# Sharing the 96-wide tails of gate and up between one full tile and a two-column-tile rest, in an attention plus GeGLU kernel on one core

## Chip, cores and metric

One core of a Trainium2 chip. The metric is the device time in microseconds (us) of one execution. Every run carries a state: fast, or slow when the granted TensorE clock was lower. A "ratio" is the mean time of one kernel's fast runs over the mean of the other's fast runs in the same rounds, so it is not quite the ratio of the medians that are quoted beside it. Intervals are 95%.

## The reference

```python
# x: 1 x 2048 x 512 bf16; 32 heads of 16; window of 8 keys, every second one; Df = 1376
xn = layernorm(x)                                   # no gain, no bias
q, k, v = split(xn @ wqkv)
attn = softmax(mask(q . k[pos - {0,2,...,14}]) / 4) # 8 logits for each position and head
a = (attn . v[same positions]) @ wo
g, u = xn @ w_gate, xn @ w_up                       # 2048 x 1376 each
out = x + a + (gelu_tanh(g) * u) @ w_down
```

The 1376 hidden columns are ten tiles of 128 and a tail of 96. The tail is what the change is about.

## The kernel before

The program is a list of tasks (engine, priority, what it reads and writes). A list scheduler at build time puts them into one static order for each engine, so a changed priority can move work that the change does not touch. The 2048 rows are four blocks of 512. Here are the parts that the argument needs, cut.

```python
# weights: gate and up whole (1376 columns), down in 10 tiles and a 96-row tail
Wg = sb("Wg", [128, 4, DF], BF);  Wu = sb("Wu", [128, 4, DF], BF)
Wd = sb("Wd", [128, NJ, 512], BF)                      # NJ = 11
# ... loads on the queue of the SP engine ...

for j in range(NJ):                                    # per block b of 512 rows
    M = 128 if j < 10 else DF - 1280                   # 96 in the tail
    # PE: gate and up, four 512-column matmuls each, into one PSUM bank each
    for kt in range(4):
        e.matmul(PS[0:M, bank], lhsT=Wx[:, kt, j*128:j*128+M], rhs=xnT[:, slot, kt, :],
                 start=(kt == 0), stop=(kt == 3))
    # ACT: gelu(gate) -> GG, copy of up -> UU;  DVE: HT[j] = GG * UU
    # all of them with priority fb + j
# ...
# down projection of row tile ti: 4 matmuls of Wo on the attention output, 11 of Wd
for j in js:
    K = 128 if j < 10 else DF - 1280
    e.matmul(PS[:, bank], lhsT=HT[0:K, slot, j, rows], rhs=Wd[0:K, j, c0:c1], ...)
# first row tile of a block: tiles 0..7 in one task, 8..10 in a second one
ja, jb = list(range(8)), list(range(8, NJ))
G.order_after(t_a, t_of["fu%d_10" % b])                # behind the last tail of up
```

Four other pieces:

```python
# DVE, LayerNorm: the second step of a tile (XIN is scaled in place), bf16 to bf16
e.tensor_scalar(out=XIN[...], in0=XIN[...], scalar1=rstd[...], ..., op0=ALU.mult)
# SP queue: the normalised x of the next blocks is transposed by DMA
e.dma_start_transpose(xnT[:, slot, :, o:o+128], XIN[:, slot, t2, :])           # "trx"
# SP queue: softmax weights go out to memory and come back in another layout
e.dma_start(pt_scratch..., PB...)                                             # "ss", 4 stores
e.dma_start(PT[...], pt_scratch...)                                           # "sl", 1 load
# DVE: PVS = BS (values) * PT;  PE: sums of PVS over heads with 32-wide column tiles ("value group")
```

Of the kernel before, what the change touches and what calls it, by code (L numbers as in the profile page):

```python
# [647 lines left out]
def d_mm(n, cnt=1):  # L648
    return cnt * max(64, n) * 0.4167e-3


def d_act(n):
    return 0.16 + 0.00085 * n
# [10 lines left out]
def bass_parallel_sum__sliding_local_dilated__glu_gated_geglu__prompt_kernel(nc, A_x, A_wqkv, A_wo, B_x, B_w_gate, B_w_up, B_w_down, out, dbg=None, cfg=None):  # L664
# [3 lines left out]
    NQT = cfg.get("NQT", 2)  # L668
    NXT = cfg.get("NXT", 3)
    NPROD = cfg.get("NPROD", 4)  # L670
    JA = cfg.get("JA", 8)
    NMS = cfg.get("NMS", 2)
    NDE = cfg.get("NDE", 1)
    NPB = cfg.get("NPB", 1)
# [25 lines left out]
    NJ = 11  # L700
# [4 lines left out]
    with contextlib.ExitStack() as es:  # L705
        block = es.enter_context(nc.Block())

        def sb(name, shape, dt):
            return es.enter_context(nc.sbuf_tensor(name, shape, dt))

        Wqkv = sb("Wqkv", [128, 4, 1536], BF)
        Wg = sb("Wg", [128, 4, DF], BF)
        Wu = sb("Wu", [128, 4, DF], BF)
        Wd = sb("Wd", [128, NJ, 512], BF)
        Wo = sb("Wo", [128, 4, 512], BF)
        xnT = sb("xnT", [128, NXT, 4, 512], BF)
# [83 lines left out]
        I_VD = Item("VD")  # L800
        I_PD = Item("PD")
        I_out = Item("out")

        PC = -1000
        PC2 = cfg.get("PC2", 8)
# [17 lines left out]
               rd=[I_E8f], wr=[I_E8], prio=PC2)  # L823
        G.task("pool", "c_zpad", 0.1, lambda e: e.memset(zpad[:, :], 0.0), wr=[I_zpad], prio=PC2)
        G.task("pool", "c_ktpad", 0.15, lambda e: e.memset(KT[:, :, 0:16], 0.0), wr=[(I_KT, "pad")], prio=PC2)
        G.task("pool", "c_e4a", 0.3, lambda e: e.tensor_tensor(
            out=E4f[:, :], in0=cf[:, 0:32], in1=cf[:, 32:64], op=ALU.add), rd=[I_cf], wr=[I_E4f], prio=PC2)
        G.task("pool", "c_e4b", 0.3, lambda e: e.tensor_tensor(
# [31 lines left out]
        for i, nm in enumerate(("q", "k", "v")):  # L860
# [2 lines left out]
                    Wqkv[:, :, i * 512:(i + 1) * 512],  # L863
                    A_wqkv[:, i * 512:(i + 1) * 512].rearrange("(k p) n -> p k n", p=128))
            t_ld["w" + nm] = G.task("sp", "ld_w" + nm, 0, mk(), wr=[(I_wq, nm)], prio=-900 + i, nbytes=512 * 1024)
        WCH = cfg.get("WCHUNK", [11])
        wch_of = {}
        j0 = 0
        for ci, nj in enumerate(WCH):
            c_lo = j0 * 128  # L870
            c_hi = min(DF, (j0 + nj) * 128)
            for j in range(j0, j0 + nj):
                wch_of[j] = ci
            for (nm, Wx, I_w, src) in (("g", Wg, I_wg, B_w_gate), ("u", Wu, I_wu, B_w_up)):
                def mk(Wx=Wx, src=src, c_lo=c_lo, c_hi=c_hi):
                    return lambda e: e.dma_start(
                        Wx[:, :, c_lo:c_hi], src[:, c_lo:c_hi].rearrange("(k p) n -> p k n", p=128))
                t_w = G.task("sp", "ld_w%s%d" % (nm, ci), 0, mk(), wr=[(I_w, ci)], prio=R_WG + 2 * ci + (nm == "u"),
                       nbytes=(c_hi - c_lo) * 1024)
                t_w.deps.add(t_ld["wk"])  # L880
                t_ld[nm] = t_w
            j0 += nj
        t_w = G.task("sp", "ld_wd0", 0, lambda e: e.dma_start(
            Wd[:, 0:10, :], B_w_down[0:1280, :].rearrange("(j p) n -> p j n", p=128)),
            wr=[(I_wd, 0)], prio=R_WD, nbytes=1280 * 1024)
        G.order_after(t_w, t_ld["u"])
        t_w2 = G.task("sp", "ld_wd1", 0, lambda e: e.dma_start(
            Wd[0:96, 10, :], B_w_down[1280:1376, :]), wr=[(I_wd, 1)], prio=R_WD + 1, nbytes=96 * 1024)
        G.order_after(t_w2, t_w)
        for d4 in range(4):  # L890
            def mk(d4=d4):
# [134 lines left out]
        for b in range(NB):  # L1026
# [264 lines left out]

            it_ht = Item("ht%d" % b, P_ht, "ht")
            fb = FFN_BASE + b * FFN_STEP
            for j in range(NJ):
                M = 128 if j < 10 else DF - 1280
                it_g = Item("g%d_%d" % (b, j), P_ps, "ffn")
                it_u = Item("u%d_%d" % (b, j), P_ps, "ffn")
                it_gg = Item("gg%d_%d" % (b, j), P_gg, "gg")
                it_uu = Item("uu%d_%d" % (b, j), P_uu, "uu")
                for (nm, Wx, I_w, it_p) in (("g", Wg, I_wg, it_g), ("u", Wu, I_wu, it_u)):  # L1300
                    def mk_f(Wx=Wx, it=it_p, j=j, M=M, itx=XTI[b]):
                        def f(e):
                            ins = None
                            for kt in range(4):
                                ins = e.matmul(PS[0:M, 512 * it.slot:512 * it.slot + 512],  # L1305
                                               lhsT=Wx[:, kt, j * 128:j * 128 + M], rhs=xnT[:, itx.slot, kt, :],
                                               start=(kt == 0), stop=(kt == 3))
                            return ins
                        return f
                    t_of["f%s%d_%d" % (nm, b, j)] = G.task("pe", "f%s%d_%d" % (nm, b, j), d_mm(512, 4), mk_f(),  # L1310
                           rd=[XTI[b], (I_w, wch_of[j])], wr=[it_p], prio=fb + j,
                           mode="f")

                def mk_gl(it=it_g, ito=it_gg, M=M):
                    return lambda e: e.activation(  # L1315
                        out=GG[0:M, ito.slot, :], in_=PS[0:M, 512 * it.slot:512 * it.slot + 512],
                        func=ACTF.Gelu_apprx_tanh)
                t_of["gelu%d_%d" % (b, j)] = G.task("act", "gelu%d_%d" % (b, j), d_act(512), mk_gl(), rd=[it_g], wr=[it_gg], prio=fb + j,
                       table="gelu")

                def mk_ue(it=it_u, ito=it_uu, M=M):
                    return lambda e: e.activation(  # L1322
                        out=UU[0:M, ito.slot, :], in_=PS[0:M, 512 * it.slot:512 * it.slot + 512], func=ACTF.Identity)
                G.task("act", "uev%d_%d" % (b, j), d_act(512), mk_ue(), rd=[it_u], wr=[it_uu], prio=fb + j)

                def mk_h(ig=it_gg, iu=it_uu, ito=it_ht, j=j, M=M):
                    return lambda e: e.tensor_tensor(  # L1327
                        out=HT[0:M, ito.slot, j, :], in0=GG[0:M, ig.slot, :], in1=UU[0:M, iu.slot, :], op=ALU.mult)
                G.task("dve", "h%d_%d" % (b, j), d_dve(512, 0.52), mk_h(), rd=[it_gg, it_uu], wr=[(it_ht, j)],
                       prio=fb + j)  # L1330

            for ti in range(4):
                t = 4 * b + ti
# [7 lines left out]
                for ci, (c0, c1) in enumerate(cparts):  # L1341
# [5 lines left out]
                    def mk_acc(js, wo, stop, ti=ti, it=it_acc, ith=it_ht, ito=it_ot, c0=c0, c1=c1, CW=CW):  # L1347
                        def f(e):
# [3 lines left out]
                                               lhsT=OT[:, ito.slot, dq, ti * 128:(ti + 1) * 128],  # L1352
                                               rhs=Wo[:, dq, c0:c1], start=(dq == 0), stop=False)
                            for j in js:
                                K = 128 if j < 10 else DF - 1280
                                ins = e.matmul(PS[:, 512 * it.slot:512 * it.slot + CW],  # L1356
                                               lhsT=HT[0:K, ith.slot, j, ti * 128:(ti + 1) * 128],
                                               rhs=Wd[0:K, j, c0:c1], start=False, stop=(stop and j == js[-1]))
                            return ins
                        return f  # L1360
                    acc_kw = dict(mode="f", util=CW / (CW + 128.0))
                    if ti == 0:
                        ja, jb = list(range(JA)), list(range(JA, NJ))
                        t_a = G.task("pe", "acca" + sfx, d_mm(CW, 4 + len(ja)), mk_acc(ja, True, False),
                               rd=[(it_ht, j) for j in ja] + [I_wd, it_ot, I_wo], wr=[it_acc],
                               prio=base + 60, **acc_kw)
                        G.order_after(t_a, t_of["fu%d_10" % b])
                        G.task("pe", "accb" + sfx, d_mm(CW, len(jb)), mk_acc(jb, False, True),
                               rd=[(it_ht, j) for j in jb] + [I_wd, it_acc], wr=[it_acc],
                               prio=base + 59.5, **acc_kw)  # L1370
# [82 lines left out]
```

## Time and profile before

| | before |
|---|---|
| time, median of 3 runs | 201.35 us (201.34 to 201.56) |
| span of the profiled run, granted clock | 199.7 us, 1.000 |
| busy: PE, DVE, ACT, POOL | 194.4, 149.2, 104.7, 10.4 us |
| longest wait of PE after the first 8 us | 0.5 us, near 92 us |

A line of a timeline reads: start in us, length in us, engine, source line, operation, what is written from what is read, tile of PE (contracted rows by output columns), moving operand, count. A bracket gives the idle time just before and what ended it. Lengths of matmuls are modelled, so PE is read from one start to the next. The prediction below shows the lines that carry its argument. One more stretch is from PE's timeline: the one hole.

```profile
91.40 1.03 PE L1305 MATMUL PS<-xnT,Wg 128*128 128x512 bf16 x4
92.89 1.05 PE L1274 MATMUL PS<-PVS,E 128*32 128x512 bf16 x16 [0.46 <-ACT UU L1322]
94.03 0.61 PE L1151 MATMUL PS<-PROD,E 128*32 128x512 bf16 x8
```

From 91.40 to 92.89 is 1.49 us for a group that needs 0.86 and a switch of 0.10. From 92.89 to 94.03 is 1.14 us for 16 matmuls that need 0.87. So 0.53 us (0.46 of it is the idle time in the bracket) and 0.27 us are lost here.

The second is VectorE's timeline in the start, where nothing but LayerNorm of the first rows can run:

```profile
9.05 0.35 DVE L972 TENSOR_SCALAR XIN<-XIN,rstd 128x512 bf16<-128x512 bf16 x1
...
10.59 0.35 DVE L972 TENSOR_SCALAR XIN<-XIN,rstd 128x512 bf16<-128x512 bf16 x1
```

These are the scalings of the third and fourth row tile, 0.35 us each. PE's first matmuls read what they write.

### The profile page before, as it was taken

The page shows a single profiled execution, that of the slowest core. Times are in us where ns is not written, and L with a number is a line of the kernel's source. Part 1 is how long each engine was busy: PE and PEld are TensorE (multiplying, and loading weights), DVE is VectorE, ACT ScalarE, POOL GpSimd, SP SyncE. Part 2 cuts the span into 40 slices and gives each one's busy share as a digit, 9 for nine tenths or more (in the row PEclk, how much of TensorE's full clock was granted, in tenths as well). Part 3 has the DMA queues.
Part 4 walks back from the last instruction along what each step waited for, and adds up shares of the span by engine and source line. Part 5 has one row for each costly group of instructions (what it writes and reads, how often), then busy time and mean ns, then how long its engine had stood idle before and what let it go on. Part 6 is the DMA issues. An engine that isn't in the chain of part 4 may idle for free.

```text
span 199.7 us, 3150 instructions
## 1 busy us (share of the span) xinstructions
PE 194.4 (97%) x1192; PEld 89.5 (45%) x1192; DVE 149.2 (75%) x230; ACT 104.7 (52%) x171; POOL 10.4 (5%) x32
## 2 busy tenths in 40 slices
PE   7899999999999999998999999999999999999994
PEld 2694344444443444443344444333444444444483
DVE  3889999889998997699996529999792986222231
ACT  4477469775667302677563036874892007767000
POOL 6520010101000010000000000000000000000000
PEclk9999999999999999999999999999999999999999
DMA  5999998898659426355931244377112440010121
GB/s 146 360 402 375 276 102 170 210 256 144 184 144 218 50 93 144 119 141 151 216 76 53 82 133 105 95 163 167 53 38 67 119 121 26 0 53 5 37 81 41
DMA packets 33055, 27.03 MB, mean 135 GB/s; under 512 B 9392, under 2 KB 31504, under 8 KB 33040
## 3 DMA queue, kind: packets, MB, share of 16 engines
q1 hardware_dynamic: 33040, 26.83, 53.8%
q8 instruction: 9, 0.15, 0.3%
q14 instruction: 6, 0.05, 0.1%
HBM read 19.99 MB, written 5.26 MB: 126 GB/s over the span
## 4 chain that ended last, share of the span: by engine, by line
PE 93%; DMA 2%; ACT 2%; DVE 1%; SPq 1%; issue 0%; DVEq 0%
PE PS L1305 37%; PE PS L1356 19%; PE PS L1089 17%; PE PS L1351 7%; PE PS L1151 4%; PE PS L1274 4%; PE PS L1045 3%; DMA XIN<-in_A_x_dram 2%; ACT L1315 1%; ACT OT L1285 1%; ACT UU L1322 0%; PE PS L997 0%; SPq L910 0%; DVE st L925 0%; ACT GG L1315 0%
## 5 line engine op out<-in xcount | busy, mean ns | idle before, releaser
L1305 PE MATMUL PS<-xnT,Wu 128*128 128x512 bf16 (+1 forms) x176 | 45.2, 380 | 0.0
L1305 PE MATMUL PS<-xnT,Wg 128*128 128x512 bf16 (+1 forms) x176 | 45.1, 379 | 0.0
L1356 PE MATMUL PS<-Wd,HT 128*128 128x512 bf16 (+3 forms) x198 | 41.3, 356 | 0.0
L1255 DVE TENSOR_TENSOR PVS<-BS,PT 128x2048 bf16<-128x2048 bf16 x32 | 37.1, 1216 | 4.2 <-DMA PT<-pt_scratch 3.5
L1135 DVE TENSOR_TENSOR PROD<-QT,KT 128x2048 bf16<-128x2048 bf16 x32 | 36.9, 1216 | 0.5 <-ACT KT L1106 0.3
L1089 PE MATMUL PS<-xnT,Wqkv 128*128 128x512 bf16 x160 | 35.9, 379 | 0.0
L1315 ACT ACTIVATE GG<-PS 128x512 bf16<-128x512 f32 (+1 forms) x44 | 26.5, 602 | 15.5 <-PE PS L1305 11.8
L1322 ACT ACTIVATE UU<-PS 128x512 bf16<-128x512 f32 (+1 forms) x44 | 26.5, 602 | 9.8 <-PE PS L1305 9.5
L1327 DVE TENSOR_TENSOR HT<-GG,UU 128x512 bf16<-128x512 bf16 (+1 forms) x44 | 17.2, 417 | 15.5 <-ACT UU L1322 15.5
L1356 PEld LDWEIGHTS PS<-Wd,HT 128*128 128x128 bf16 (+1 forms) x198 | 19.4, 98 | 18.7
L1305 PEld LDWEIGHTS PS<-xnT,Wg 128*128 128x128 bf16 (+1 forms) x176 | 17.1, 100 | 21.6 <-issue 2.5
L1305 PEld LDWEIGHTS PS<-xnT,Wu 128*128 128x128 bf16 (+1 forms) x176 | 16.6, 100 | 22.9 <-issue 3.4
L1376 DVE TENSOR_TENSOR OB<-PS,XR 128x512 bf16<-128x512 f32 (+1 forms) x18 | 11.3, 628 | 19.7 <-PE PS L1356 18.5
L1089 PEld LDWEIGHTS PS<-xnT,Wqkv 128*128 128x128 bf16 x160 | 15.4, 98 | 19.0 <-issue 0.4
L1351 PE MATMUL PS<-Wo,OT 128*128 128x512 bf16 (+1 forms) x72 | 16.8, 355 | 0.0
L1285 ACT ACTIVATE OT<-PS 128x512 bf16<-128x512 f32 x16 | 8.7, 595 | 15.3 <-PE PS L1274 15.3
L1106 ACT ACTIVATE KT<-PS 128x512 bf16<-128x512 f32 x12 | 7.2, 597 | 13.3 <-PE PS L1089 13.3
L1099 ACT ACTIVATE QT<-PS 128x512 bf16<-128x512 f32 x12 | 7.2, 596 | 12.8 <-PE PS L1089 12.6
L925 DVE BATCH_NORM_STATS2 st<-XIN 128x6 f32<-128x512 bf16 x16 | 10.7, 685 | 3.7 <-DMA XIN<-in_A_x_dram 3.7
L1113 ACT ACTIVATE VT<-PS 128x512 bf16<-128x512 f32 x16 | 9.6, 598 | 4.7 <-PE PS L1089 4.7
L942 POOL TENSOR_TENSOR sq<-ve,mhalf 128x2 bf16<-128x2 f32 (+1 forms) x10 | 6.7, 666 | 68.5 <-DVE ve L936 68.5
L1351 PEld LDWEIGHTS PS<-Wo,OT 128*128 128x128 bf16 x72 | 6.9, 97 | 7.2 <-issue 0.4
(53 smaller groups left out, 117.1 us busy)
## 6 DMA issues: line engine op xcount, KB each, us to landing
BS<-vt_scratch SPq DMA_DIRECT2D x64, 128.5 KB, 3.1
vt_scratch<-VT SPq DMA_DIRECT2D x16, 128.0 KB
XR<-in_A_x_dram SPq DMA_DIRECT2D x16, 128.0 KB, 2.1
XIN<-in_A_x_dram SPq DMA_DIRECT2D x7, 256.0 KB, 6.1
out_dram<-OB SPq DMA_DIRECT2D x14, 128.0 KB, 2.0
Wqkv<-in_A_wqkv_dram SPq DMA_DIRECT2D x3, 512.0 KB, 4.2
Wg<-in_B_w_gate_dram SPq DMA_DIRECT2D x1, 1376.0 KB
Wu<-in_B_w_up_dram SPq DMA_DIRECT2D x1, 1376.0 KB, 11.2
```

The costliest lines, as they stand in the source:

```text
L925: return lambda e: e.bn_stats(out=st[:, t, :], in_=XIN[:, it.slot, t2, :])
L1089: ins = e.matmul(PS[:, 512 * it.slot:512 * it.slot + HWD], lhsT=lhsT, rhs=xnT[:, itx.slot, kt, c0:c0 + HWD], start=(kt == 0), stop=(kt == 3))
L1135: return lambda e: e.tensor_tensor(out=PROD[:, it.slot, :, :], in0=bass.AP(QT, (itq.slot * 4 + g) * 512, [[NQT * 4 * 512, 128], [0, 4], [1 ...
L1255: return lambda e: e.tensor_tensor(out=bass.AP(PVS, (ito.slot * 2 + half) * 2048, [[NPVS * 4096, 128], [512, 4], [128, 4], [1, 128]]), in0 ...
L1285: return lambda e: e.activation(out=OT[:, ito.slot, dq, :], in_=PS[:, 512 * it.slot:512 * it.slot + 512], func=ACTF.Identity)
L1305: ins = e.matmul(PS[0:M, 512 * it.slot:512 * it.slot + 512], lhsT=Wx[:, kt, j * 128:j * 128 + M], rhs=xnT[:, itx.slot, kt, :], start=(kt = ...
L1315: return lambda e: e.activation(out=GG[0:M, ito.slot, :], in_=PS[0:M, 512 * it.slot:512 * it.slot + 512], func=ACTF.Gelu_apprx_tanh)
L1322: return lambda e: e.activation(out=UU[0:M, ito.slot, :], in_=PS[0:M, 512 * it.slot:512 * it.slot + 512], func=ACTF.Identity)
L1327: return lambda e: e.tensor_tensor(out=HT[0:M, ito.slot, j, :], in0=GG[0:M, ig.slot, :], in1=UU[0:M, iu.slot, :], op=ALU.mult)
L1351: ins = e.matmul(PS[:, 512 * it.slot:512 * it.slot + CW], lhsT=OT[:, ito.slot, dq, ti * 128:(ti + 1) * 128], rhs=Wo[:, dq, c0:c1], start=( ...
L1356: ins = e.matmul(PS[:, 512 * it.slot:512 * it.slot + CW], lhsT=HT[0:K, ith.slot, j, ti * 128:(ti + 1) * 128], rhs=Wd[0:K, j, c0:c1], start ...
L1376: return lambda e: e.tensor_tensor(out=OB[:, ito.slot, 0:CW], in0=PS[:, 512 * it.slot:512 * it.slot + CW], in1=XR[:, itx.slot, c0:c1], op= ...
```

## The change

Intent: a 96-wide tile costs PE as much as a 128-wide one. Gate's 96 tail columns and 32 of up's fill one full tile. Up's other 64 columns are a rest, which is run as two 64-wide column tiles side by side, each on half of the 512 rows. That is meant to take half a group's time. The tail is given its turn after the fifth pair of tiles instead of at the end. The tail of the down weights lies in rows 32 to 127, so that its hidden values stand at the partitions where the products leave them; 32 rows of zeros fill it up.

```diff
+        Wt = sb("Wt", [128, 4, 192], BF)              # gate tail 96 + up 32 | up 64
+        G.task("pool", "c_wdz", ..., lambda e: e.memset(Wd[0:32, 10, :], 0.0), prio=PC2 + 20)
+        G.task("pool", "c_htz", ..., lambda e: e.memset(HT[0:32, :, 10, :], 0.0), prio=PC2 + 20)
...      # three loads for Wt behind those of Wg and Wu, which shrink to 1280 columns
-            Wd[0:96, 10, :], B_w_down[1280:1376, :]
+            Wd[32:128, 10, :], B_w_down[1280:1376, :]
...
-            for j in range(NJ):
+            for j in range(NJ - 1):
...
+                    for kt in range(4):                # full tail tile, priority fb + 4.5
+                        e.matmul(PS[:, bank], lhsT=Wt[:, kt, 0:128], rhs=xnT[:, slot, kt, :], ...)
+                    for kt in range(4):                # rest, priority fb + 4.5
+                        for c in range(2):
+                            e.matmul(PS[64*c:64*c+64, 256 columns], lhsT=Wt[:, kt, 128:192],
+                                     rhs=xnT[:, slot, kt, 256*c:256*c+256], tile_position=(0, 64*c))
+                # ACT: one gelu over all 128 partitions; no copy of up's tail
+            for (nm, p0, n, g0, c0, c1, it_s) in (("a", 0, 32, 32, 0, 512, it_g),
+                                ("b", 0, 64, 64, 0, 256, it_u), ("c", 64, 64, 64, 256, 512, it_u)):
+                    # DVE: HT[g0:g0+n, 10, c0:c1] = GG[g0:g0+n, c0:c1] * PS[p0:p0+n, ...]
...
-                                K = 128 if j < 10 else DF - 1280
-                        ja, jb = list(range(JA)), list(range(JA, NJ))
+                        ja, jb = [0, 1, 2, 3, 4, 5, 6, 7, 10], [8, 9]
-                        G.order_after(t_a, t_of["fu%d_10" % b])
+                        G.order_after(t_a, t_of["fu%d_9" % b])
```

## The prediction

> **What bounds the kernel now.** I read the page's busy shares first, then the chain of work that ended last, then the longest waits, then each engine's timeline.
>
> ```profile
> PE 194.4 (97%) x1192; PEld 89.5 (45%) x1192; DVE 149.2 (75%) x230; ACT 104.7 (52%) x171; POOL 10.4 (5%) x32
> ...
> PE 93%; DMA 2%; ACT 2%; DVE 1%; SPq 1%; issue 0%; DVEq 0%
> ```
>
> TensorE is busy for 97% of the span and is 93% of the chain. A busy PE is no proof by itself, because matmul ends are modelled, so the waits of PE have to be looked at:
>
> ```profile
> PE PS L853 <- POOL wsrc L806: 1.4, 1, 1.4
> PE PS L1045 <- ACT xnT L1008: 0.5, 1, 0.5
> PE PS L1274 <- ACT UU L1322: 0.5, 1, 0.5
> PE PS L997 <- DVE XIN L972: 0.2, 1, 0.2
> ```
>
> These are all the waits of PE: 2.6 us, and 2.1 us of them lie in the first 8 us. From then until the last matmul at 197 us the PE stream has one hole of 0.5 us, near 92 us. So the time is decided by how many PE slots the kernel issues and by what a switch between two kinds of matmul costs. Both are read from start-to-start times in PE's timeline:
>
> ```profile
> 19.87 1.90 PE L1305 MATMUL PS<-xnT,Wg 128*128 128x512 bf16 x8
> 21.70 0.62 PE L1151 MATMUL PS<-PROD,E 128*32 128x512 bf16 x8
> 22.25 1.04 PE L1305 MATMUL PS<-xnT,Wg 128*128 128x512 bf16 x4
> ...
> 38.24 1.03 PE L1305 MATMUL PS<-xnT,Wu 128*128 128x512 bf16 x4
> 39.10 1.03 PE L1305 MATMUL PS<-xnT,Wg 128*96 128x512 bf16 x4
> 39.96 1.03 PE L1305 MATMUL PS<-xnT,Wu 128*96 128x512 bf16 x4
> 40.83 6.21 PE L1089 MATMUL PS<-xnT,Wqkv 128*128 128x512 bf16 x28
> ```
>
> Three readings. A full group of four 512-column matmuls takes 39.10 - 38.24 = 0.86 us, 216 ns each. The two 96-wide tail groups take 0.86 and 0.87 us: a tail that is a quarter narrower costs exactly as much as a full tile. And eight matmuls on 32-wide column tiles start at 21.70 and give way at 22.25, 0.55 us: at 216 ns each one after the other they would need 1.73 us, so four of them run side by side and the pure streaming is two rounds, 0.43 us.
>
> **The price of a switch.** From 19.87 to 22.25 is 2.38 us for eight full matmuls (1.73) and those two rounds (0.43): the rest, 0.22 us, is going to column tiles and back, about 0.10 in and 0.12 out.
>
> **What the Trainium skill says.** (1) "TensorEngine Tiling (Array Packing)", section Key Properties: a change of the tiling mode drains the TensorE, while different tiles execute in parallel. The trace agrees in both: 0.22 us for the two changes, and four abreast. It has no case of two 64-wide tiles, which the change uses. (2) "TensorE: Matmul & The Clock Gate", section "Step-by-step: what each phase is for": weight loading scales with the column count and the row count doesn't matter. So padding the down tail from 96 to 128 rows should be free; the trace has 381 ns for the 96-row down matmul and 379 for the 128-row one, 98 ns for both weight loads. (3) "VectorE: DVE Perf Modes", section "What auto-detection actually checks": the packed 2x mode needs every tensor to be 16-bit. The trace agrees: the 512-element product of two bf16 tiles takes 417 ns, the 512-element add with an f32 PSUM operand 687 ns. (4) "DMA: Bandwidth & Descriptors", Specifications: at least 512 B for line rate. The new tail loads have rows of 192, 64 and 128 B; no row of the trace before isolates what such a load costs.
>
> ```profile
> L1327 DVE TENSOR_TENSOR HT<-GG,UU 96x512 bf16<-96x512 bf16 x4 | 1.7, 418 | 2.6 <-ACT UU L1322 2.6
> L1376 DVE TENSOR_TENSOR OB<-PS,XR 128x512 bf16<-128x512 f32 x14 | 9.6, 687 | 15.2 <-PE PS L1356 15.1
> L1376 DVE TENSOR_TENSOR OB<-PS,XR 128x256 bf16<-128x256 f32 x4 | 1.7, 424 | 4.6 <-PE PS L1356 3.4 <-DMA out_dram<-OB 1.2
> L1322 ACT ACTIVATE UU<-PS 96x512 bf16<-96x512 f32 x4 | 2.4, 592 | 0.9 <-PE PS L1305 0.8
> ```
>
> **The change part by part, for each of the four blocks.**
> PE, removed: eight 96-wide matmuls of 512 columns, 8 x 0.216 = 1.73 us. PE, added: one full group (gate's 96 columns and 32 of up), 4 x 0.216 = 0.86 us, and eight matmuls of 64 columns x 256 elements on two column tiles. If the pair runs side by side, that is four rounds at half of 0.216 (the 256-wide down matmuls come 15 in 1.64 us, 109 ns each, so halving the length does halve the pitch): 0.44 us. Plus two mode switches, 0.22 us, unless the group lands next to another column-tiled group; then those switches are paid already. Net: 1.73 - 0.86 - 0.44 - 0.22 = 0.21 us saved where the rest stands alone, 0.43 where it has a tiled neighbour.
> Where will it stand? It has its turn after the fifth pair of gate and up. In block 0 (about 30 us) and in block 3 (about 172 us) the neighbours are full matmuls: 2 x 0.21. In block 1 (about 63 us) and block 2 (about 139 us) the small logit groups of the next block are interleaved there, so a shared switch is possible: 2 x 0.21 to 2 x 0.43. Sum 0.84 to 1.28 us; I take 1.0 us. All of it lies on the path, as PE has no idle time to hide it in.
> ACT: four copies of up's tail go (4 x 0.59 = 2.4 us of 104.7). ACT is 52% busy and mostly waits for PE, so worth nothing by itself.
> DVE: per block one 418 ns product goes; three with a PSUM operand come, estimated from the add's rows as 687 + 2 x 424 = 1535 ns. +1.12 us per block, +4.5 us in all, to about 154 us (77%). Off the path in total, not necessarily at the place.
> Down projection: same number of matmuls, same pitch: 0. Two memsets on POOL (5% busy): 0. Doing the tail early and leaving tiles 8 and 9 to the end removes no wait, since before there is no PE wait at that seam: in block 3 the down matmuls follow the last up tail at 0.86 us.
> Loads: three more issues at some 0.45 us each on the queue at about 9 us, 1536 short rows, no more bytes. The tail is wanted only at about 30 us. Hidden.
>
> **The rivals.**
> Rival A, PSUM held longer. Before, ACT empties both banks of a pair (0.6 us each). Now both banks of the tail stay until DVE has multiplied out of them, and three banks are allowed to gate and up. DVE has long runs of higher-ranked work: in block 1 it makes no gate-up product between 42.6 and 62.2 us. In the trace before ACT's four spare buffers absorb that; banks can't. With one bank left, a gate or up group would come every 0.86 + 0.27 + 0.60 = 1.7 us instead of 0.86, so each 2 us of hold loses about 1 us of PE, unless projections of the next block can be drawn in. Against: in block 0 and 1 there is such other work, in block 3 DVE is nearly idle (a product each 1.73 us), and the static order is made with these holds known. Most at risk is block 2, near 139 to 144 us, where PE has only gate and up matmuls and DVE has the softmax steps. Estimated cost 0 to 2 us; I put 0.3 us into the centre. With all of it: 201.5 to 202.
> Rival B, no overlap of the two 64-wide tiles. Then eight matmuls at 109 ns are 0.87 us and nothing is saved while switches are paid: +0.22 x 4 = +0.9 us, time 202.2. Against: the 32-wide tiles run four abreast with different moving data.
> Rival C, the short rows delay the big weights and x loads behind them. DMA is at 360 to 402 GB/s in slices 2 to 4; if the tail weights landed after 30 us or the second block's x came over 3 us later, PE would stall by 1 to 2 us: about 202. I give it little.
> Rival D, the reshuffled order removes the 0.5 us hole near 92 us and shares more switches: about 199.7. Other holes may come instead.
>
> **Range and chances.** 201.35 - 1.0 + 0.3 = 200.65, so I predict 200.6 us. The best case (1.28 saved, 0.5 of the hole gone) gives 199.6; a hold that costs 1.5 us, or B, gives 201.9 to 202.2. The 8-in-10 range is 199.7 to 202.0. Faster by 2% needs 197.3, more than all removable PE work: 2%. Slower by 2% needs 205.4, several stalls of microseconds: 4%. Within: 94%.
>
> **What the profile after would show.** The rest group: eight 64x256 matmuls between starts 0.54 to 0.56 us apart (0.44 plus the way out), with the group ahead of it 0.10 longer; at about 1.0 us Rival B is right. The three products near 0.69, 0.42 and 0.42 us. PE's waits still under 3 us; a new PE wait on a bank held by a product near 139 to 145 us would be Rival A, one on tail weights at about 30 us Rival C. DVE near 154 us, ACT near 102 us. The prediction is wrong if the other PE groups change their pitch, or if PE gets more than 1.5 us of new waits.

## The result

| | before | changed |
|---|---|---|
| median, same rounds | 201.45 us (201.34 to 201.89, 4 runs) | 201.05 us (200.80 to 203.84, 4 runs, one of them slow) |
| span of the profiled run | 199.7 us | 199.1 us |
| busy PE, DVE, ACT, POOL | 194.4, 149.2, 104.7, 10.4 us | 192.9, 154.3, 102.9, 12.9 us |
| start of first gate group | 18.36 us | 18.66 us |
| first gate group to last PE group | 177.32 us | 176.48 us |

The ratio is 0.9972, interval 0.9948 to 0.9995. The run of 203.84 us had a granted clock of 0.992 and is left out. The same kernel gave 201.00 us against 201.84 us, ratio 0.9961 (0.9934 to 0.9988). It was run at another time. The last two rows of the table are starts read from PE's timeline; they split the 0.5 us in a useful way: the start got slower by 0.3 us and the rest faster by 0.84 us.

The page of the changed kernel, busy times and chain of work:

```profile
PE 192.9 (97%) x1208; PEld 88.4 (44%) x1208; DVE 154.3 (78%) x238; ACT 102.9 (52%) x167; POOL 12.9 (6%) x34
...
PE 74%; DVE 13%; DMA 6%; SPq 3%; issue 2%; POOL 0%; DVEq 0%
```

The busy shares look the same as before, but the chain does not: PE carried 93% of it and now carries 74%, with VectorE, transfers and the DMA-issuing queue in the rest. Some stretch is now decided off PE. The list of PE's waits, 3.6 us in sum against 2.6 before, shows which:

```profile
PE PS L858 <- POOL wsrc L809: 1.4, 1, 1.4
PE PS L1277 <- DVE PVS L1258: 0.9, 1, 0.9
PE PS L1048 <- ACT xnT L1011: 0.5, 1, 0.5
PE PS L1000 <- DVE XIN L972: 0.5, 1, 0.5
PE PS L1000 <- DVE XIN L975: 0.3, 1, 0.3
```

All but the second lie in the first 8 us. The second is new: 0.9 us in which PE waits for VectorE's products of values and softmax weights.

**Where PE's work shrank.** PE's timeline around the tail of block 0, and around the rest of block 1:

```profile
29.91 1.03 PE L1343 MATMUL PS<-xnT,Wt 128*128 128x512 bf16 x4
30.86 0.63 PE L1355 MATMUL PS<-xnT,Wt 128*64 128x256 bf16 x8
31.42 0.82 PE L1308 MATMUL PS<-xnT,Wg 128*128 128x512 bf16 x3
...
45.25 1.03 PE L1092 MATMUL PS<-xnT,Wqkv 128*128 128x512 bf16 x4
46.20 0.63 PE L1355 MATMUL PS<-xnT,Wt 128*64 128x256 bf16 x8
46.76 0.61 PE L1154 MATMUL PS<-PROD,E 128*32 128x512 bf16 x8
47.31 1.25 PE L1092 MATMUL PS<-xnT,Wqkv 128*128 128x512 bf16 x5
```

In block 0 the tail takes from 29.91 to 31.42, 1.51 us; before it was 1.73 (eight matmuls of 216 ns). That is 0.22 us saved. The rest itself is 0.56 us, which is 0.44 of streaming and 0.12 of switching, so its two halves do run side by side. In block 1 the full tile does not come until 89.85, but the scheduler has drawn the rest forward to 46.20, in front of a 32-wide logit group. The switch in from full matmuls is paid once for both. Yet the rest still takes 0.56 us up to the start of the logit group. Going from 64-wide to 32-wide tiles costs 0.12 us as well. Net in such a place: 1.73 - 0.86 - 0.56 = 0.31 us. The rests of blocks 2 and 3 stand at 90.81 and 167.09 in front of 32-wide value groups, also 0.56 us. Sum: 0.22 + 3 x 0.31, about 1.14 us (the terms are rounded).

**What the products cost.** The groups of instructions by form:

```profile
L1371 DVE TENSOR_TENSOR HT<-GG,PS 64x256 bf16<-64x256 bf16 x8 | 3.4, 420 | 0.2
L1371 DVE TENSOR_TENSOR HT<-GG,PS 32x512 bf16<-32x512 bf16 x4 | 2.7, 677 | 0.5 <-ACT GG L1364 0.4
```

677 and twice 420 ns make 1.52 us a block.

**What the start lost.** POOL's timeline, then VectorE's, of the changed kernel:

```profile
8.73 0.94 POOL L830 MEMSET HT<- 32x1024 bf16 x1
```

```profile
9.07 0.75 DVE L975 TENSOR_SCALAR XIN<-XIN,rstd 128x512 bf16<-128x512 bf16 x1
...
10.99 0.35 DVE L975 TENSOR_SCALAR XIN<-XIN,rstd 128x512 bf16<-128x512 bf16 x1
```

The same scaling that took 0.35 us at 9.05 now takes 0.75 us at 9.07 and ends at 9.82, just after the fill has ended at 9.67. From the first statistics of the third row tile (6.67 before, 6.68 now) to the scaling of the fourth it is 3.92 us before and 4.31 us now.

**What PE now waits for.** Three timelines of the changed kernel around 86 us. The DMA-issuing queue:

```profile
73.38 1.78 SPq L1225 DMA_DIRECT2D pt_scratch<-PB  x4
75.21 0.45 SPq L1427 DMA_DIRECT2D out_dram<-OB  x1
75.70 2.50 SPq L984 DMA_TRANSPOSE xnT<-XIN  x2
78.39 0.43 SPq L1232 DMA_DIRECT2D PT<-pt_scratch  x1
```

VectorE:

```profile
81.49 2.36 DVE L1258 TENSOR_TENSOR PVS<-BS,PT 128x2048 bf16<-128x2048 bf16 x2 [2.93 <-DMA out_dram<-OB]
```

PE:

```profile
82.63 2.75 PE L1092 MATMUL PS<-xnT,Wqkv 128*128 128x512 bf16 x12
86.27 1.05 PE L1277 MATMUL PS<-PVS,E 128*32 128x512 bf16 x16 [0.89 <-DVE PVS L1258]
...
91.36 1.05 PE L1277 MATMUL PS<-PVS,E 128*32 128x512 bf16 x16
92.34 0.82 PE L1092 MATMUL PS<-xnT,Wqkv 128*128 128x512 bf16 x3
```

The softmax weights are stored from 73.38 on and loaded back by the issue at 78.39. Between them stand two transposes, which hold the queue for 2.50 us and are for a later block. VectorE sits idle for 2.93 us until the load has landed. (The bracket names an output store; the profile gives the wait to whichever transfer ended last before the start, and the run "pt_load_first" below shows that the load is the one that counts.) PE reaches the value group 0.89 us too early. Before, the same load stood behind the same two transposes and was issued at 80.34, but the value group had its place at 87.83 and PE had projections to do until then. The last two lines show that the old holes near 92 us are gone: 91.36 to 92.34 is 0.98 us, which is 0.87 and the way out.

The working hypothesis was therefore this sum, in us from the first gate group to the last PE group: tail work -1.14, old holes -0.53 and -0.27, new hole +0.94 (from start to start; 0.89 is its idle time), two new small holes (62.22 and 149.50) +0.12 and +0.13. That is -0.75; measured -0.84, so 0.09 is not assigned. With +0.3 from the start this is the -0.5 of the profiled pair. The runs below test each term.

### The profile page after: what moved, and what is told of

It is laid out like the page before. It is cut to its first block, busy times and chain, and to the rows that moved or that the text cites. A ratio compares the mean times of both kernels' runs of the same rounds, so it can differ in the third digit from the quotient of the medians.

```text
span 199.1 us, 3195 instructions
## 1 busy us (share of the span) xinstructions
PE 192.9 (97%) x1208; PEld 88.4 (44%) x1208; DVE 154.3 (78%) x238; ACT 102.9 (52%) x167; POOL 12.9 (6%) x34
## 4 chain that ended last, share of the span: by engine, by line
PE 74%; DVE 13%; DMA 6%; SPq 3%; issue 2%; POOL 0%; DVEq 0%
PE PS L1308 31%; PE PS L1400 14%; PE PS L1092 12%; DVE PVS L1258 6%; PE PS L1396 5%; PE PS L1154 3%; PE PS L1277 3%; DMA XIN<-in_A_x_dram 2%; DMA xnT<-XIN 2%; DVE PROD L1138 2%; PE PS L1048 2%; PE PS L1343 2%; DMA out_dram<-OB 1%; SPq L984 1%; DVE OB L1420 1%
## 5 line engine op out<-in xcount | busy, mean ns | idle before, releaser
L1400 PE MATMUL PS<-Wd,HT 128*128 128x512 bf16 (+1 forms) x198 | 41.1, 355 | 0.0
L1308 PE MATMUL PS<-xnT,Wg 128*128 128x512 bf16 x160 | 41.0, 380 | 0.0
L1308 PE MATMUL PS<-xnT,Wu 128*128 128x512 bf16 x160 | 41.0, 379 | 0.0
L1318 ACT ACTIVATE GG<-PS 128x512 bf16<-128x512 f32 x40 | 24.0, 600 | 13.1 <-PE PS L1308 11.9
L1325 ACT ACTIVATE UU<-PS 128x512 bf16<-128x512 f32 x40 | 24.0, 599 | 9.2 <-PE PS L1308 9.1
L1400 PEld LDWEIGHTS PS<-Wd,HT 128*128 128x128 bf16 x198 | 19.4, 98 | 18.7
L1330 DVE TENSOR_TENSOR HT<-GG,UU 128x512 bf16<-128x512 bf16 x40 | 15.9, 420 | 13.0 <-ACT UU L1325 12.6
L1308 PEld LDWEIGHTS PS<-xnT,Wu 128*128 128x128 bf16 x160 | 15.1, 98 | 20.2 <-issue 2.1
L1308 PEld LDWEIGHTS PS<-xnT,Wg 128*128 128x128 bf16 x160 | 14.8, 98 | 20.6 <-issue 2.7
L928 DVE BATCH_NORM_STATS2 st<-XIN 128x6 f32<-128x512 bf16 x16 | 10.4, 683 | 3.7 <-DMA XIN<-in_A_x_dram 3.7
L945 POOL TENSOR_TENSOR sq<-ve,mhalf 128x2 bf16<-128x2 f32 (+1 forms) x10 | 7.7, 772 | 63.5 <-DVE ve L939 63.5
```

The lines of the kernel that those rows point to most:

```text
L928: return lambda e: e.bn_stats(out=st[:, t, :], in_=XIN[:, it.slot, t2, :])
L1308: ins = e.matmul(PS[0:M, 512 * it.slot:512 * it.slot + 512], lhsT=Wx[:, kt, j * 128:j * 128 + M], rhs=xnT[:, itx.slot, kt, :], start=(kt = ...
L1318: return lambda e: e.activation(out=GG[0:M, ito.slot, :], in_=PS[0:M, 512 * it.slot:512 * it.slot + 512], func=ACTF.Gelu_apprx_tanh)
L1325: return lambda e: e.activation(out=UU[0:M, ito.slot, :], in_=PS[0:M, 512 * it.slot:512 * it.slot + 512], func=ACTF.Identity)
L1330: return lambda e: e.tensor_tensor(out=HT[0:M, ito.slot, j, :], in0=GG[0:M, ig.slot, :], in1=UU[0:M, iu.slot, :], op=ALU.mult)
L1400: ins = e.matmul(PS[:, 512 * it.slot:512 * it.slot + CW], lhsT=HT[:, ith.slot, j, ti * 128:(ti + 1) * 128], rhs=Wd[:, j, c0:c1], start=Fal ...
```

## The experiments

All runs gave correct results; all were timed in five rounds against the kernel before. Each of the three calls below ran on another chip, so runs of different calls are compared by their ratios. "First gate to last" is the time from the start of the first gate group to that of the last PE group, from PE's timeline of the profiled run. It leaves out the first 18 to 20 us, where the arrival of x and of the first weights scatters by some tenths from run to run. It is one execution for each kernel. Two profiles of the changed kernel gave 176.48 and 176.54.

| run | median, us | ratio to before (95%) | first gate to last, us |
|---|---|---|---|
| first call, before 201.71 | | | |
| e1_rest_untiled | 201.70 | 0.9997 (0.9981 to 1.0013) | 177.02 |
| e2_zeros_later | 201.42 | 0.9991 (0.9969 to 1.0013) | 176.68 |
| e3_rest_32wide | 201.13 | 0.9969 (0.9952 to 0.9987) | 176.22 |
| e4_both | 201.11 | 0.9973 (0.9954 to 0.9992) | 176.43 |
| second call, before 201.84 | | | |
| e5_changed_again | 201.00 | 0.9961 (0.9934 to 0.9988) | 176.54 |
| e6_before_with_zeros | 202.10 | 1.0010 (0.9981 to 1.0038) | 177.39 |
| e7_hole_closed | 201.60 | 0.9998 (0.9967 to 1.0029) | 176.25 |
| e8_position_only | 201.36 | 0.9976 (0.9949 to 1.0003) | 176.79 |
| third call, before 201.62 | | | |
| e9_pt_load_first | 200.18 | 0.9921 (0.9902 to 0.9939) | 175.50 |
| e10_all_three | 200.25 | 0.9929 (0.9905 to 0.9952) | 175.27 |
| e11_shared_tail_last | 200.29 | 0.9928 (0.9911 to 0.9944) | 175.72 |
| e12_rest_not_drawn_ahead | 203.13 | 1.0060 (1.0041 to 1.0079) | 177.56 |

### e1: the rest without column tiles

```diff
-                        for c in range(2):
-                            e.matmul(PS[64*c:64*c+64, 256 columns], lhsT=Wt[:, kt, 128:192],
-                                     rhs=xnT[:, slot, kt, 256*c:256*c+256], tile_position=(0, 64*c))
+                        e.matmul(PS[0:64, 512 columns], lhsT=Wt[:, kt, 128:192],
+                                 rhs=xnT[:, slot, kt, :], ...)
```

> The changed kernel in exactly its own order on every engine, but up's remaining 64 columns run as four ordinary matmuls of 512 elements instead of eight 256-element ones on two column tiles; the products read the same values. Theory (the gain is the side-by-side pair, less what the mode switches cost): each rest grows from 0.44 us to 0.86 us, and the switch goes: +0.21 us in block 0, where it stands alone, +0.30 us in blocks 1 to 3, where the neighbour is a 32-wide group whose own switches stay. Sum +1.1 us: about 202.1 us against 201.0 for the changed kernel, so some 0.5 us slower than the kernel before. Rival (the gain comes from the new order and from less ScalarE work, not from the tiling): time unchanged, about 201.0 us.

Measured: 201.70 us, ratio 0.9997. PE's timeline around the rest of block 0:

```profile
30.64 1.03 PE L1343 MATMUL PS<-xnT,Wt 128*128 128x512 bf16 x4
31.60 1.05 PE L1354 MATMUL PS<-xnT,Wt 128*64 128x512 bf16 x4
32.58 1.04 PE L1308 MATMUL PS<-xnT,Wg 128*128 128x512 bf16 x4
```

The rest takes 0.98 us instead of 0.56, and the same 0.98 us at 47.36, in front of a logit group. The edit did less than was expected of it: the switch did not go. The full tile ahead of the rest takes 0.96 us (0.86 and 0.10 in), and the rest 0.86 and 0.12 out. So a matmul of 64 columns pays the switch even with no second tile beside it; the 96-wide tails of the kernel before (0.86 and 0.87 us) did not. The run thus isolates the side-by-side pair better than planned: it is worth 0.42 us a rest. From the first value group of block 1 (the one with the new hole) to the last PE group it is 109.59 us against 108.87, 0.72 more: two dearer rests, 0.84, less the small hole at 149.50, which this run does not have. Over the whole stretch from the first gate group, however, only 0.5 us was lost, and the time rose less than expected. The reason is in the same timeline: the value group of block 1 came at 86.83 without a wait. Work added before 86 us only filled the hole. This was the first sign that PE did not set the pace in the stretch up to 86 us, whatever its busy share said.

### e2: the zero fills later

```diff
-        G.task("pool", "c_wdz", ...)                   # at the start of POOL's work
-        G.task("pool", "c_htz", ...)
+        G.order_after(G.task("pool", "c_wdz", ...), t_of["sq3"])   # behind LayerNorm's last
+        G.order_after(G.task("pool", "c_htz", ...), t_of["sq3"])   # square root of the first rows
```

> The changed kernel, but the two zero fills on POOL come after the fourth normalisation step of the first block instead of before it; every other engine has the same order. Theory: the 0.94 us fill of the hidden tile made VectorE's normalisation take 0.75 us instead of 0.35 us and that late start of 0.3 to 0.4 us is carried to the end. Then the normalisation is back at 0.35 us, the first small logit group starts near 19.3 us (19.62 in the changed kernel, 19.32 in the kernel before), and the time falls by 0.3 us to about 200.7 us. Rival (the late start comes from the extra loads of the tail weights, or is swallowed by a later wait): the normalisation stays long or the time stays at 201.0 us.

Measured: 201.42 us, ratio 0.9991. The scaling is back at 0.35 us and the stretch of the start at 3.93 us (4.31 in the changed kernel), so the theory of the fills holds in the trace. The total did not gain: the hole at the value group of block 1 grew from 0.89 to 1.10 us, and in this profile the third row tile of x came 0.34 us later (first statistics at 7.02 us, not 6.68). What is saved ahead of a wait on another engine is given back in the wait. The fills did not come behind the fourth scaling, as the expectation has it, but beside it (10.67 to 12.22 us); here that scaling took 0.39 us, in e10 it took far longer.

### e3: the rest on four 32-wide column tiles

```diff
-                        for c in range(2):             # two 64-wide tiles
+                        for c, w, q in ((0, 128, 0), (0, 160, 1), (1, 128, 2), (1, 160, 3)):
+                            e.matmul(PS[32*q:32*q+32, 256 columns], lhsT=Wt[:, kt, w:w+32],
+                                     rhs=xnT[:, slot, kt, 256*c:256*c+256], tile_position=(0, 32*q))
```

> The changed kernel in its own order, but the rest runs as sixteen matmuls on four 32-wide column tiles instead of eight on two 64-wide ones, same pattern of 256 elements, same result. Theory: the change from 64-wide to 32-wide tiles is itself a mode switch of 0.12 us, paid three times; with 32-wide tiles it vanishes: rest groups next to a logit or value group take 0.43 us instead of 0.56, in sum -0.37 us, about 200.65 us. The rest of block 0, which stands alone, stays at 0.55 us. Rival (what is left after the group is a drain that any next group pays): no change in length, 201.0 us. A second rival: twice as many matmuls cost issue time and the groups get longer.

Measured: 201.13 us, ratio 0.9969. PE's timeline of the same place:

```profile
46.74 0.62 PE L1355 MATMUL PS<-xnT,Wt 128*32 128x256 bf16 x16
47.19 0.60 PE L1154 MATMUL PS<-PROD,E 128*32 128x512 bf16 x8
```

Sixteen matmuls of half the width take 0.45 us to the logit group's start, against 0.56 for eight 64-wide ones. The streaming is the same, so the 0.11 us was the change from 64-wide to 32-wide tiles; with one width in both groups it is gone. Behind the hole, where two rests lie, the gain arrives: 108.63 us against 108.87, twice 0.12. Before the hole it does not.

### e4: e2 and e3 together

> The two edits together: zero fills later and the rest on 32-wide tiles. If both losses are real and lie on the path they add: -0.7 us against the changed kernel, about 200.3 us, 0.5 per cent under the kernel before. If one is swallowed by the wait near 86 us, about 200.6 us.

The edits are those of the two runs above. Measured: 201.11 us, ratio 0.9973, the same as e3 alone and above what the sum of the two would give. The hole at 86.71 us is 1.08 us long. So what was gained before it, at the start and in the rest at 46 us, did not come out behind it. A sum of parts is no prediction while a wait stands behind them.

### e5: the changed kernel again

> The changed kernel unaltered, as the reference for the other runs on one chip: ratio to the kernel before 0.997 as in the first measurement, with the wait of some 0.9 us before the value group near 86 us and the long normalisation of 0.75 us near 9 us.

Nothing is edited. Measured: 201.00 us, ratio 0.9961, a hole of 0.95 us. It gives the yardstick of the second call, and says that the hole belongs to the kernel and not to one profile.

### e6: the zero fills in the kernel before

```diff
+        G.task("pool", "c_wdz", ..., lambda e: e.memset(OT[0:32, 0, 0, :], 0.0), prio=PC2 + 20)
+        G.task("pool", "c_htz", ..., lambda e: e.memset(OT[0:32, 1, 0:2, :], 0.0), prio=PC2 + 20)
```

The fills write a buffer that is overwritten before anyone reads it, with the size and the place in POOL's order of those of the change.

> The kernel before, to which only two zero fills on POOL of the same sizes and at the same place in POOL's order are added, into a tile that is not in use yet; all other engines keep their order. Theory (the fills hold up VectorE's normalisation on the path): the normalisation goes from 0.35 to 0.75 us, PE's first gate group comes 0.35 us later, and, as PE has only one small hole later on, most of it stays: +0.3 us, ratio 1.0015. Rival (the late start in the changed kernel was from the new loads): no change, ratio 1.000.

Measured: 202.10 us against 201.84, ratio 1.0010 with an interval that includes no change. The time alone does not decide it. The trace does. POOL's timeline, then VectorE's:

```profile
8.94 0.94 POOL L827 MEMSET OT<- 32x1024 bf16 x1
```

```profile
9.28 0.75 DVE L974 TENSOR_SCALAR XIN<-XIN,rstd 128x512 bf16<-128x512 bf16 x1
```

The scaling takes 0.75 us beside the fill in this kernel too, and ends at 10.03, 0.15 us after the fill (9.88). In the changed kernel it was also 0.15 us. Everything else of the kernel before is unchanged, so the fill alone does this. The Trainium skill has the mechanism: "SBUF — State Buffer", section "SBUF: two separate sides", says that VectorE and GpSimd share one port pair, that it is an exclusive lock and no split of bandwidth, and that a VectorE instruction in a 2-port mode and a GpSimd instruction block each other for the whole instruction. The trace agrees: the scaling ends 0.15 us after the fill in three kernels, whatever its own start, with lengths of 0.75 us here and 1.51 us in e12. It works both ways: in e2 the second fill met a scaling that was already running and took 1.09 us instead of 0.94. And it is not all of VectorE's work: in e2 two statistics (BATCH_NORM_STATS2) ran largely beside that fill in 1.27 us, as long as without one (1.28). No run shows the mode of the scaling itself. The prediction did not look this page up and put the fills at 0.

### e7: the value group moved behind two more projection groups

```diff
+        # in PE's order: the first value group of block 1 behind the last two groups of its
+        # neighbour projection; ACT's two copies of its result likewise; on top of e4
+        later("pe", "pvr1_1", "mm2_2_3_0")
+        later("act", "evo1_0", "evv2_3_0"); later("act", "evo1_1", "evo1_0")
```

> The version with later zero fills and 32-wide rests, in which the first value group of the second block is moved behind the last two projection groups of the third (and its two ScalarE copies likewise). Nothing else changes its order. Theory (the wait of 0.9 to 1.1 us near 86 us swallows what the change gains before it, and a better order gets it back): the wait goes; VectorE finishes the next value products only near 91 us, so about 0.3 us of wait comes back at the second value group: -0.6 us against the version with the two edits, ratio to the kernel before 0.994. Rival (what ends at 91 us is a chain of VectorE and DMA that sets the time anyway): the wait moves to the second value group, time unchanged, ratio 0.997.

Measured: 201.60 us with a wide scatter (200.87 to 202.54), ratio 0.9998. PE's timeline:

```profile
87.33 1.05 PE L1277 MATMUL PS<-PVS,E 128*32 128x512 bf16 x16
...
91.54 1.05 PE L1277 MATMUL PS<-PVS,E 128*32 128x512 bf16 x16 [0.78 <-DVE PVS L1258]
```

The first value group has no wait any more, and the second one waits 0.78 us for VectorE. The rival had the wait right, but neither forecast had the time (0.994 or 0.997). Moving PE's work around did not help here: VectorE's whole run of value products is late. So its start has to be moved.

### e8: the new order alone, with the old 96-wide tails

```diff
+                pj = fb + (4.5 if j == 10 else j)      # priority of all tail tasks
-                        ja, jb = list(range(JA)), list(range(JA, NJ))
-                        G.order_after(t_a, t_of["fu%d_10" % b])
+                        ja, jb = [0, 1, 2, 3, 4, 5, 6, 7, 10], [8, 9]
+                        G.order_after(t_a, t_of["fu%d_9" % b])
```

> The kernel before with only the position changed: the old 96-wide tail takes its turn after the fifth pair, and tiles 8 and 9 go last into the down projection. Theory (the position frees no PE work, there was no PE wait at the end of a block): within 0.4 us of the kernel before, the sign decided by where the new order happens to wait; ratio 0.998 to 1.002. Rival (the position is the gain): ratio 0.997 or less, like the whole change.

Measured: 201.36 us, ratio 0.9976, at the edge of what was expected; the interval (0.9949 to 1.0003) covers the theory and the rival, so the time does not decide between them. PE's timeline near the old hole:

```profile
91.64 1.03 PE L1306 MATMUL PS<-xnT,Wg 128*128 128x512 bf16 x4
92.61 1.05 PE L1274 MATMUL PS<-PVS,E 128*32 128x512 bf16 x16
93.74 0.62 PE L1151 MATMUL PS<-PROD,E 128*32 128x512 bf16 x8
```

91.64 to 92.61 is 0.97 us: the 0.46 us wait of the kernel before is gone without any new tile shape. The 0.27 us in front of the logit group (92.61 to 93.74 is 1.13 us) stays. First gate to last is 176.79 us against 177.32, 0.53 less. So in the trace a part of the changed kernel's gain comes from the order and not from the tiles, in the size of the hole.

### e9: the load of the softmax weights ahead of the two transposes

```diff
+        # changed kernel; in the DMA queue's order only:
+        later("sp", "trx6_1", "sl1"); later("sp", "trx6_0", "sl1")
```

> The changed kernel; only in the DMA queue the load of the second block's softmax weights is moved ahead of two transposes of the fourth block's x, which stand before it and are not wanted for another 20 us. Theory (the wait of 0.9 us before the value group near 86 us is the DMA queue's order: the weights were stored by 77 us, but their load is issued only at 78.4 us, behind 2.5 us of transposes): the load is issued near 77.1 us, VectorE's value products start at 80.1 us instead of 81.5, the wait of 0.9 us goes, nothing takes its place: -0.9 us against the changed kernel, ratio to the kernel before 0.992. Rival (the wait comes from VectorE's own work or from the windows of v): no change, 0.996.

Measured: 200.18 us, ratio 0.9921 (0.9902 to 0.9939). The DMA-issuing queue, VectorE's timeline, PE's timeline and PE's waits:

```profile
75.27 0.45 SPq L1427 DMA_DIRECT2D out_dram<-OB  x1
76.58 0.34 SPq L1232 DMA_DIRECT2D PT<-pt_scratch  x1
76.97 2.50 SPq L984 DMA_TRANSPOSE xnT<-XIN  x2
```

```profile
79.60 3.50 DVE L1258 TENSOR_TENSOR PVS<-BS,PT 128x2048 bf16<-128x2048 bf16 x3 [0.97 <-DMA PT<-pt_scratch]
```

```profile
85.38 1.05 PE L1277 MATMUL PS<-PVS,E 128*32 128x512 bf16 x16
86.36 1.90 PE L1092 MATMUL PS<-xnT,Wqkv 128*128 128x512 bf16 x8
```

```profile
PE PS L858 <- POOL wsrc L809: 1.4, 1, 1.4
PE PS L1048 <- ACT xnT L1011: 0.3, 1, 0.3
```

The load is issued 1.81 us earlier, VectorE starts its products 1.89 us earlier, and the value group follows the projections without a wait. The bracket now names the load itself. First gate to last is 175.50 us, 0.98 less than in the changed kernel: that is the hole (0.94 from start to start), all but 0.04; the two small holes are still there (1.07 us at 61.21, 0.99 at 147.61). No other instruction changed its place on any engine, so the hole came from the place of this load in the queue, as the theory said. The transposes come 1.27 us later, and nobody waits for them. PE's share of the chain is back at 93%. Both kernels are beaten. Of the versions tried, e9, e10 and e11 are the best, and their intervals do not tell them apart.

### e10: e9 with the zeros later and the 32-wide rest

> The same queue move on the version with later zero fills and 32-wide rests. Theory: with the wait gone, the 0.39 us of the fills and the 0.3 us of the tile widths are no longer swallowed: 0.6 us below the run before it, 200.0 us or less, ratio to the kernel before 0.989 to 0.992. Rival: another chain takes over and the time equals that of the run before it.

Measured: 200.25 us, ratio 0.9929. The part after the first gate group did gain, 175.27 us against 175.50, but that is 0.23 us, and the total shows nothing of the 0.4 us of the start. In this profile the first gate group begins at 19.16 us, later than in e9 (18.74), because PE waited 0.75 us for the first projection weights to arrive. So the expected gain of this run is not shown in the time. The trace shows two more things. The edit did not take the fills out of VectorE's way: they fell beside the fourth scaling, which took 1.27 us instead of 0.35 (PE did not wait for it in this profile):

```profile
10.57 1.27 DVE L973 TENSOR_SCALAR XIN<-XIN,rstd 128x512 bf16<-128x512 bf16 x1
```

And the chain of work is off PE again: PE carries 71% of it and VectorE 20%, most of the latter from 16.5 to about 62 us. That fits the rival, another chain that takes over. Whether the start can gain at all stays open.

### e11: the shared tail at the end of the block

```diff
-    JT = cfg.get("JT", 4.5)
-    JLATE = cfg.get("JLATE", [8, 9])
+    JT = cfg.get("JT", 10)
+    JLATE = cfg.get("JLATE", [8, 9, 10])
```

> The changed kernel with the shared tail back at the end of the block (tail after tile 9, tiles 8, 9 and the tail last in the down projection). Theory (sharing makes the gain, position only shifts where PE waits): same PE work as the changed kernel, since three rests again find a tiled neighbour; within 0.5 us of the changed kernel, ratio to the kernel before 0.994 to 0.999. Rival (mid block is needed for the sharing to pay, as the products out of PSUM hold up the end of the block): a new PE wait of over 0.5 us between the last up group and the down projection, ratio 1.000 or more.

Measured: 200.29 us, ratio 0.9928, better than either side of the question had it. The first value group of block 1 comes at 87.61 us with no wait, and PE has no wait but those of the first 10 us. First gate to last is 175.72 us. The place in mid block is thus not needed for the gain. It is even what put the value group too early: with the tail at the end of the block, the static order has the group later and the load of the weights, issued at 79.42 us, is in time.

### e12: the rest tied behind its own full tile

```diff
+            G.order_after(t_of["fu%d_10" % b], t_of["fg%d_10" % b])
```

> The changed kernel with each rest tied behind its own full tile, so that it cannot be drawn ahead into an earlier tiled stretch, where it holds a PSUM bank for up to 57 us. Theory (holding the bank costs nothing here): two more rests stand alone, 0.1 us each: +0.2 us on PE against the changed kernel, plus or minus what the new order waits. Rival (the third bank is missed): PE waits on ScalarE fall by over 0.3 us and the time is lower.

In the changed kernel the rest of block 1 runs at 46 us and its bank is read out much later, behind the full tile at 90 us. This run takes that away. Measured: 203.13 us, ratio 1.0060: worse by 2 us than the changed kernel. Two parts, of about the same size, can be read. The first is in the start. POOL's timeline, then VectorE's:

```profile
9.39 0.52 POOL L829 MEMSET Wd<- 32x512 bf16 x1
9.85 0.94 POOL L830 MEMSET HT<- 32x1024 bf16 x1
```

```profile
9.43 1.51 DVE L975 TENSOR_SCALAR XIN<-XIN,rstd 128x512 bf16<-128x512 bf16 x1
```

In this build both fills fell beside the scaling, which took 1.51 us and again ended 0.15 us after the last fill (10.94 against 10.79). That is 0.76 us more than in the changed kernel; the x tile came 0.36 us later as well, and the first gate group begins 1.13 us later. The second part is in PE's timeline:

```profile
87.80 1.05 PE L1277 MATMUL PS<-PVS,E 128*32 128x512 bf16 x16 [1.10 <-DVE PVS L1258]
...
92.61 1.05 PE L1277 MATMUL PS<-PVS,E 128*32 128x512 bf16 x16 [0.50 <-DVE PVS L1258]
```

Two waits for value products, 1.6 us instead of 0.9; the rests of blocks 2 and 3 now stand alone between full matmuls (0.1 us each), and one more wait of 0.16 us came. Together about 1.1 us, and first gate to last is 177.56 us, 1.08 more than in the changed kernel. No wait of PE on ScalarE fell away in exchange, so the bank held for some 50 us cost nothing that can be seen. So of the 2 us only about 0.2 is the rest's own place; the others are waits and fills that came with the new order. As a test of the held bank the run is not clean for that reason.

## Why the prediction was right, and where its terms were off

The total was right: 200.6 us predicted, 201.05 and 201.00 us measured, within 2% and inside the range. The mechanism of the saving was right too; that the sum came so near was in part luck, because the start, the old holes and the new ones come to +0.3 - 0.8 + 1.2 = +0.7 us, where +0.3 stood for something else. Step by step:

1. *PE is the bound; the time is PE slots and switches.* Right for most of the span. It no longer holds between about 49 and 86 us of the changed kernel, where the chain runs over VectorE and the DMA queue (e1, e2 and e4: what was added or saved there did not reach the end). The sign "PE's waits still under 3 us" was missed: they are 3.6 us; the limit of 1.5 us of new waits was kept (1.0).
2. *Tail saving 1.0 us (0.84 to 1.28).* The mechanism was right and the size near: 1.14 us. The pair runs side by side (0.56 us where e1 takes 0.98, both with the way out), so Rival B falls. Two errors nearly cancel. A tiled neighbour was to save 0.43 us; it saves 0.31, as 64-wide to 32-wide is itself a switch of 0.12 us (e3). But three rests found such a neighbour and not two at most, because the scheduler drew them forward.
3. *The three products near 0.69, 0.42 and 0.42 us, VectorE at about 154 us.* Right: 677, 420 and 420 ns, 154.3 us; ScalarE 102.9 us where 102 was named. *Padding the down tail is free*: the trace shows no change in the 379 ns of such a matmul.
4. *Two fills on POOL: 0.* This step failed. The start lost 0.39 us in VectorE and 0.3 us at the first gate group, because a fill of 0.94 us held up a scaling (e6 shows it in the kernel before, e2 takes it away). POOL's low busy share says nothing about whom its instructions hold up.
5. *Loads hidden.* Right. The three issues of tail weights took 0.79, 2.05 and 2.07 us and not 0.45, and the last two transfers landed 7.7 and 9.7 us after their issue, but no PE wait on them is in the trace, and the first use is at 29.91 us. Rival C falls.
6. *Rival A, PSUM held, 0.3 us in the centre.* It did not occur: PE has no wait on a bank held by a tail product. A cost of about that size was there, but for another reason that no rival named: a transfer issued behind transposes, late value products and a 0.89 us hole (e9). So +0.3 stood in the sum for the wrong thing: that is luck. A slip besides: with all of the 2 us of Rival A the prediction's own sum gives 201.35 - 1.0 + 2.0 = 202.35, not 201.5 to 202.
7. *Rival D, the 0.5 us hole goes and others may come.* Right in both halves: gone by the order alone in e8, and a longer one came at 86 us.

The centre's -1.0 + 0.3 = -0.7 us thus became -1.14 in the tails, -0.80 in old holes, +1.19 in new ones and +0.3 in the start: about -0.45 us; the medians moved by 0.40 and 0.84. The split is from single profiles, and 0.09 us of it is not assigned.

## What to carry to other kernels

In a kernel whose PE is busy for 97%, a saving on PE reaches the end only if the next chain off PE is not waiting just behind it: after such a change read the chain of work again, and where its PE share has dropped (93% to 74% here), look in the issue order of the DMA queue for an urgent load behind work that is not urgent. Moving one load past two transposes gained about as much again as the whole change did (ratio 0.9921 with both, 0.9972 and 0.9961 with the change alone, each against the kernel before). Small fills on an idle engine were not free next to a latency chain of VectorE, and column tiles of two widths side by side still paid a switch.

## What the Trainium skill lacked or had wrong

- "TensorEngine Tiling (Array Packing)", Key Properties: it says that a change of mode drains the TensorE, but gives no time. Measured: about 0.10 us into column tiles, 0.12 us out, 0.11 us from 64-wide to 32-wide, which the page lists as separate configurations. It does not say that a 64-column matmul alone pays the change too: 0.10 us in and 0.12 us out in e1, and none for 96 columns.
- The same page has no measured case of two 64-wide tiles: eight 64-wide matmuls of 256 columns, two abreast, stream in 0.44 us, and sixteen 32-wide ones, four abreast, in 0.45 us.
- "DMA: Bandwidth & Descriptors": its section on DMA transposes gives no time for which one holds the issuing queue on this chip. Measured: 1.25 us each for 128 KB in most pairs (2.50 us for two), against 0.34 to 0.45 us for most plain transfers. While the big weight loads were under way, some plain transfers held it longer too: 2.05 and 2.07 us for the two loads of up's tail columns, but also 6.93 us for one load of x in the kernel before, so short rows are not shown to be the reason.
- "SBUF — State Buffer" has the lock between VectorE and GpSimd, and the runs agree with it. It lacks a case with a GpSimd fill: a scaling of 128x512 bf16 took 0.35 us alone, 0.75 us beside a fill of 0.94 us and 1.51 us beside two, each time ending 0.15 us after the fill; batch-norm statistics beside a fill kept their length (1.27 us for two).
